# An expert layer's last weights: the same bytes from another queue, converted on chip, and a load cut in two around gathers

## The chip, the cores and the metric

One core of one Trainium2 chip. The metric is the device time of one execution in microseconds (us), the median of several executions. For one core a run is called slow when it is over 1.5% above the fastest run of the same kernel; otherwise it is fast. TensorE multiplies matrices, VectorE (DVE) and ScalarE (ACT) work on elements, GpSimd (POOL) issues most transfers here and SyncE (SP) some; PEld is TensorE's loading of weights.

## The reference

Attention first (left out here: the change does not touch it). Its 3072 rows of 512 then go through eight experts. Each computed row belongs to one expert, which is chosen by the data:

```python
xc = x[do_compute]
e_idx = np.argmax(xc @ w_gate, axis=1)
...
for e in range(E):
    mask = e_idx == e
    h = np.maximum(xc[mask] @ w1[e], 0.0)          # 512 -> 1024
    y[mask] = gate_w[mask, None] * (h @ w2[e])     # 1024 -> 512
out[do_compute] = xc + y
```

## The kernel before

A first weight `w1[e]` and a second weight `w2[e]` are 2 MiB each in fp32 in memory. TensorE wants them as fp16. The kernel before loads every one of them with a DMA issued by GpSimd that converts on the way. GpSimd also gathers the rows of an expert (indirect DMA) and scatters them back:

```python
def new_half(e, i, pool=wp, tags=("w1t", "w2t")):       # a place on chip for w1 or w2
    t = pool.tile([P, DS * F], FP16, tag=tags[i], name=tags[i])
    wts[e, i] = t.rearrange("p (s x) -> p s x", s=(DS, FS)[i])

def part(e, i, x):                                      # load a part of it, fp32 -> fp16
    nc.gpsimd.dma_start(out=wts[e, i][:, x], in_=(w1r, w2r)[i][e][:, x])
...
def in_parts(e, i, *to):                                # first half now, second half on call
    ...
def scatter(e, t):
    apart(nc.gpsimd.indirect_dma_start(out=out[:, :], ..., in_=xg[e, t], ...))
```

The work is cut into twelve units. The first eight are one tile of 128 rows of an expert among the first four. The last four are both tiles of experts 4 to 7 (counted from zero; "last expert" below is expert 7, "fourth expert" is expert 3). For each unit, `up_` multiplies by `w1` and applies the relu, and `down` multiplies by `w2`, then adds onto the gathered row with one VectorE instruction (the multiply-add, line L791):

```python
def down(n, then):
    ...
    todo = [(i, f) for i in range(len(ts)) for f in range(FS)]
    if n == len(units) - 1:                   # the last: start the second tile early
        todo = todo[:4] + todo[8:10] + todo[4:8] + todo[10:]
    for i, f in todo:
        ...
        nc.tensor.matmul(yps[i], hts[n][:, f, i * P:(i + 1) * P], wts[e, 1][:, f], ...)
    for i, t in enumerate(ts):
        nc.vector.scalar_tensor_tensor(xg[e, t], yps[i], tab[:, t, e, 1:2], xg[e, t], ...)
        waiting.append((e, t))                # to be scattered
```

The last second weights stand after unit 6, ahead of the scatters of all later units:

```python
        elif n == 2 * FB - 2:                 # after unit 6
            for x in waiting[2:]:
                scatter(*x)
            del waiting[2:]
            in_parts(7, 1)()                  # both halves of the last w2, one after the other
        elif n > 2 * FB - 2:
            scatters()
```

The softmax here doesn't subtract the row's maximum and nothing guards it: scores larger than these inputs give would overflow.

## Time and profile before

| | before |
|---|---|
| median of 3 runs | 189.2 us (188.47 to 189.75) |
| profiled run | 186.2 us, span 184.0, clock 0.978 |
| last first weights (w1t) landed, last up-projection starts: **T** | 164.97 |
| last second weights (w2t), second half in use | 171.45 = T + 6.5 |
| last matmul ends | 173.77 = T + 8.8 |
| last scatter starts | 176.04 = T + 11.1 |

A timeline line reads: start in us, length, engine, line of the kernel, operation, output and inputs, and in brackets how long the engine had been idle and what ended that. All times after "T +" are counted from the start of the last expert's up-projection, because T itself moves by several microseconds from run to run for reasons that have nothing to do with the change: three profiles of kernels that are alike up to T (before, e5 and e14 below) have 164.97, 167.16 and 169.75. One caution: the profiled run of before is a lucky one: 186.2 us, where the three others took 188.5 to 189.8. When the same file was profiled again (e5 below) its span was 187.0.

### The profile page before, as it was taken

Reading aid. Unit: us, or ns where it says so; the run is one execution under the profiler, and the core shown is the slowest. Engines: PE = TensorE matmul, PEld = TensorE weight load, DVE = VectorE, ACT = ScalarE, POOL = GpSimd, SP = SyncE. Lnnn points to the kernel's source line nnn. Section 1 sums busy time; section 2 is a strip of 40 time slices with the busy share of each in tenths; the row PEclk is TensorE's granted clock in tenths of the full one; section 3 lists DMA queues with packets and bytes.
Section 4 is the critical chain, followed back from the end, with each engine's and each line's share of the span. In section 5 each row is a group of like instructions: output and inputs, shape, how many; then the busy total and the mean of one; then the engine's idle time right before and its main releaser. Section 6 shows DMA issues by size and latency. Waiting matters only on the chain.

```text
span 184.0 us, 5757 instructions
## 1 busy us (share of the span) xinstructions
PE 160.0 (87%) x2443; PEld 113.6 (62%) x2443; DVE 105.8 (58%) x284; ACT 89.6 (49%) x138; POOL 95.2 (52%) x123
## 2 busy tenths in 40 slices
PE   5799878998978999999999999979999999999500
PEld 1464546676654887667878779657777676646100
DVE  5798938437666676687776437533565445343300
ACT  3068659896796848987448352213234332302000
POOL 7749731233761217732322891688787626507740
PEclk9999999999999999999999999999999999999965
DMA  5999999999999999999999999999999999999520
GB/s 173 169 183 164 163 192 203 200 235 138 224 208 223 237 233 211 165 220 235 252 230 240 319 253 222 203 233 253 216 244 201 202 239 251 218 251 221 182 87 2
DMA packets 53204, 38.16 MB, mean 207 GB/s; under 512 B 28448, under 2 KB 44832, under 8 KB 53168
## 3 DMA queue, kind: packets, MB, share of 16 engines
q0 software_dynamic: 49168, 30.62, 110.7%
q1 hardware_dynamic: 3728, 6.69, 10.7%
q8 instruction: 21, 0.34, 0.7%
q10 hardware_dynamic: 272, 0.39, 0.6%
q14 instruction: 15, 0.12, 0.2%
HBM read 56.66 MB, written 10.49 MB: 365 GB/s over the span
## 4 chain that ended last, share of the span: by engine, by line
PE 43%; DMA 24%; issue 11%; POOL 9%; DVE 5%; ACT 4%; POOLq 1%; DVEq 0%; ACTq 0%
DMA xg<-out_dram,idx 13%; DMA w2t<-in_moe_w_dram 8%; PE tps L307 5%; PE sps L344 4%; PE xps L468 4%; PE av L293 3%; PE sps L339 3%; PE tbp L562 3%; PE av L426 3%; DMA firstat<-in_q_dram 2%; PE sps L373 2%; POOL xg L715 2%; PE mhp L770 2%; PE av L432 2%; PE sps L404 2%
## 5 line engine op out<-in xcount | busy, mean ns | idle before, releaser
L460 POOL CAST x<-x 128x512 f16<-128x512 f32 x17 | 10.5, 619 | 38.7 <-DVE x L451 31.5
L355 ACT ACTIVATE at<-sps 128x1024 f16<-128x1024 f32 (+1 forms) x24 | 21.1, 923 | 8.7 <-PE sps L344 8.6
L788 PE MATMUL myp<-w2t,ht 128*128 128x512 f16 x96 | 23.8, 379 | 1.4 <-DMA w2t<-in_moe_w_dram 1.4
L726 POOL DMA_INDIRECT out_dram<-xg,idx x16 | 16.1, 1003 | 16.6 <-DMA out_dram<-xg,idx 4.8
L791 DVE SCALAR_TENSOR_TENSOR xg<-myp,tab,xg 128x512 f32<-128x512 f32 x16 | 12.0, 751 | 21.9 <-PE myp L788 20.2
L770 PE MATMUL mhp<-mxT,w1t 128*128 128x128 f16 (+1 forms) x320 | 22.9, 230 | 0.0
L770 PEld LDWEIGHTS <-w1t 128*128 128x128 f16 x320 | 21.0, 98 | 2.8 <-DMA w1t<-in_moe_w_dram 0.4
L776 ACT ACTIVATE ht<-mhp 128x512 f16<-128x512 f32 x16 | 9.6, 597 | 25.6 <-PE mhp L770 16.8
L720 POOL DMA_INDIRECT xg<-out_dram,idx x16 | 16.8, 1053 | 9.8 <-DVE rec L440 2.7
L788 PEld LDWEIGHTS <-ht 128*128 128x128 f16 x128 | 11.9, 98 | 12.0 <-issue 1.3
L774 DVE TENSOR_SCALAR ht<-mhp 128x512 f16<-128x512 f32 x16 | 11.0, 691 | 11.9 <-PE mhp L770 11.0
L344 PE MATMUL sps<-qT,kT 64*128 64x512 f16 (+3 forms) x96 | 14.6, 303 | 1.3 <-DVE kT L313 1.3
L394 ACT ACTIVATE ats<-sps 128x1024 f16<-128x1024 f32 (+1 forms) x16 | 12.5, 812 | 6.5 <-PE sps L385 6.5
L451 DVE TENSOR_TENSOR x<-av,rec 128x512 f32<-128x512 f32 x20 | 13.8, 692 | 1.5
L468 PE MATMUL xps<-ident,x 128*128 128x128 f16 (+1 forms) x96 | 11.3, 240 | 2.3 <-POOL x L460 1.7
L114 POOL DMA_DIRECT2D va<-in_v_dram x8 | 11.4, 1424 | 3.3 <-DMA va<-in_v_dram 2.0
L360 ACT ACTIVATE at<-sps 128x1024 f16<-128x1024 f32 (+1 forms) x12 | 10.8, 921 | 4.4 <-PE sps L344 4.3
L339 PE MATMUL sps<-tri,idl 64*128 64x128 f16 x144 | 11.5, 218 | 0.2
L293 PE MATMUL av<-esk,ident 128*128 128x512 f16 x28 | 9.4, 465 | 2.6 <-DVE ident L151 1.8
L313 DVE COPY kT<-tps 128x768 f16<-128x768 f16 x10 | 9.5, 948 | 3.6 <-PE tps L307 3.6
L313 ACT COPY qT<-tps 128x768 f16<-128x768 f16 x12 | 9.6, 797 | 3.6 <-PE tps L307 3.6
L426 PE MATMUL av<-va,at 128*128 128x65 f16 x204 | 9.9, 194 | 1.2 <-issue 1.2
(154 smaller groups left out, 343.1 us busy)
## 6 DMA issues: line engine op xcount, KB each, us to landing
out_dram<-x SPq DMA_DIRECT2D x24, 256.0 KB, 5.9
w1t<-in_moe_w_dram POOLq DMA_DIRECT2D x6, 1024.0 KB, 14.9
w2t<-in_moe_w_dram POOLq DMA_DIRECT2D x4, 1024.0 KB, 16.3
va<-in_v_dram POOLq DMA_DIRECT2D x8, 384.0 KB, 9.9
w2t<-in_moe_w_dram POOLq DMA_DIRECT2D x4, 512.0 KB, 13.4
qin<-in_moe_w_dram POOLq DMA_DIRECT2D x2, 1024.0 KB
kin<-in_moe_w_dram POOLq DMA_DIRECT2D x2, 1024.0 KB, 12.5
qin<-in_q_dram POOLq DMA_DIRECT2D x2, 768.0 KB, 9.2
```

The costliest lines, as they stand in the source:

```text
L293: nc.tensor.matmul(ps, ident, fill, start=True, stop=True)
L313: eng(t.rearrange("c (p n) -> c p n", n=NT), ps.rearrange("c n p -> c p n"))
L339: nc.tensor.matmul(ps[:, k, x:x + P], idl[rows[i], u], tri[rows[i], u], start=(u == 0), stop=False, skip_group_check=True)
L344: nc.tensor.matmul(ps[:, k, x:x + n], kT[b, pr][rows[i], j * P:(j + 1) * P], qT[b, pr][rows[i], q0:q0 + n], start=False, stop=True, skip_g ...
L355: nc.scalar.activation(both[b][:, :, o:o + w], ps[:, :, :w], ACT.Exp, scale=SCALE)
L426: nc.tensor.matmul(avo[:, 0, h // 2], at[b, h][:, x0:x0 + P], va[b % 2][:, h, j], start=False, stop=j == i, skip_group_check=True)
L451: nc.vector.tensor_tensor(x.rearrange("p c t d -> p t c d"), avo[:, :, :, :D], rec.unsqueeze(3).to_broadcast([P, 2, 4, D]), op=ALU.mult)
L468: nc.tensor.matmul(ps[:, s], x[:, s * P:(s + 1) * P], ident if x.dtype == FP16 else ident32, is_transpose=True, start=(s == 0), stop=(s == ...
L720: apart(nc.gpsimd.indirect_dma_start(out=xg[e, t], out_offset=None, in_=out[:n, :], in_offset=bass.IndirectOffsetOnAxis(ap=idx[:, t, e:e + ...
L726: apart(nc.gpsimd.indirect_dma_start(out=out[:, :], out_offset=bass.IndirectOffsetOnAxis(ap=idx[:, t, e:e + 1], axis=0), in_=xg[e, t], in_ ...
L770: nc.tensor.matmul(hp[:, u], wts[e, 0][:, s, (f0 + u) * P:(f0 + u + 1) * P], xts[n][:, s], start=(s == 0 and u == 0), stop=(s == DS - 1 an ...
L788: nc.tensor.matmul(yps[i], hts[n][:, f, i * P:(i + 1) * P], wts[e, 1][:, f], start=(f == 0), stop=(f == FS - 1))
```

## The change

The intent: take the last of the big loads off GpSimd's queue, so that SyncE's queue carries it and GpSimd is free to scatter. SyncE's load leaves the fp32 as it is, so it arrives in two pieces `w32` of 1 MiB and VectorE and ScalarE convert them in four copies of 128x1024 elements. This is **part B**. **Part A** is separate: the fourth expert's second weights are cut into two halves, and the second half is issued after two gathers instead of before them.

```diff
@@ down
-            todo = todo[:4] + todo[8:10] + todo[4:8] + todo[10:]
+            todo = todo[:4] + todo[8:12] + todo[4:8] + todo[12:]
@@ before the routing of the second tiles                      (part A)
-    for i in range(2):
-        load_half(3, i)
+    load_half(3, 0)
+    new_half(3, 1)
+    part(3, 1, slice(0, FS // 2))
@@ loop over the units
         down(n, ...)
+        if n == len(units) - 3:                                # (part B)
+            for i in range(2):
+                nc.vector.memset(w32[i][:, 0, :1], 0.0)
+                nc.sync.dma_start(out=w32[i],
+                                  in_=w2r[E - 1][:, i * FS // 2:(i + 1) * FS // 2])
         if n == len(units) - 2:
             up_(n + 1)
+            for f in range(0, FS, 2):
+                eng = nc.scalar.copy if f % 4 else nc.vector.tensor_copy
+                eng(wts[E - 1, 1][:, f:f + 2], w32[f * 2 // FS][:, f % (FS // 2):][:, :2])
         if n == 0:
             gather(0, 1)
             gather(1, 1)
+            part(3, 1, slice(FS // 2, FS))                     # (part A)
             load_half(4, 0, *qk)
@@ after unit 6
-            in_parts(7, 1)()
+            new_half(7, 1)
+            w32 = [m2.tile([P, FS // 2, DM], FP32, tag=f"w32{i}", name="w32", bufs=1)
+                   for i in range(2)]
```

## The prediction

> **What bounds the kernel now.** I read the page first (busy shares and slices), then the chain that ended last, then the timeline of the expert stage. In the page's slices TensorE and the DMA engines are both at nine tenths almost to the end, so the question is which of them sets the last microseconds:
>
> ```profile
> PE   5799878998978999999999999979999999999500
> DMA  5999999999999999999999999999999999999520
> HBM read 56.66 MB, written 10.49 MB: 365 GB/s over the span
> ```
>
> The chain that ended last, over the final 46 us, is one transfer after another and a short tail:
>
> ```profile
> 138.60 14.49 DMA xg<-out_dram,idx
> ...
> 156.30 15.11 DMA w2t<-in_moe_w_dram
> 171.41 0.04 issue
> 171.45 2.33 PE myp L788 x10
> 173.78 0.03 issue
> 173.81 0.76 DVE xg L791
> ...
> 176.04 0.98 POOL out_dram L726
> ```
>
> The reader is to see that the second half of the last expert's second weights (w2t) lands at 171.41, that ten matmuls wait for it, and that the last scatter starts 1.47 us after the final multiply-add has ended (173.81 + 0.76 = 174.57). The timeline shows the waits around this, as start, length, instruction, and in brackets the idle time before it:
>
> ```profile
> 123.69 0.63 PE L753 MATMUL mtp<-ident,xg 128*128 128x128 f32 x4 [1.34 <-DMA xg<-out_dram,idx]
> ...
> 164.97 3.39 PEld L770 LDWEIGHTS <-w1t 128*128 128x128 f16 x32 [0.42 <-DMA w1t<-in_moe_w_dram]
> ...
> 165.70 0.98 POOL L726 DMA_INDIRECT out_dram<-xg,idx  x1 [4.43 <-DMA out_dram<-xg,idx]
> ...
> 169.00 1.46 PE L788 MATMUL myp<-w2t,ht 128*128 128x512 f16 x6 [0.36 <-DMA w2t<-in_moe_w_dram]
> ...
> 171.45 2.32 PE L788 MATMUL myp<-w2t,ht 128*128 128x512 f16 x10 [1.00 <-DMA w2t<-in_moe_w_dram]
> ...
> 173.81 0.75 DVE L791 SCALAR_TENSOR_TENSOR xg<-myp,tab,xg 128x512 f32<-128x512 f32 x1 [0.54 <-PE myp L788]
> 174.75 0.98 POOL L726 DMA_INDIRECT out_dram<-xg,idx  x1 [0.31 <-DVE xg L791]
> 176.04 0.98 POOL L726 DMA_INDIRECT out_dram<-xg,idx  x1 [0.30 <-issue]
> ```
>
> Three readings. From 124 us to the end of the last up-projection TensorE hardly waits, so the 1.34 us wait at 123.69 for the gathered rows of unit (0,1) is its one sizeable gap there. GpSimd runs its last nine scatters back to back, 1.29 us apart, from 165.70 to 176.04 (8 x 1.29 = 10.3): it is itself a bound at the end. And the last expert's first weights (w1t) arrive just when TensorE wants them: issued 144.61, 20.3 us to landing in the DMA issues view, so 164.9.
>
> The DMA stream is full. After the third scatter ahead of it in the queue lands (issued 154.54, 11.8 us: 166.3), both halves of w2t land by 171.41: 2 MiB of fp32 in 5.1 us, 411 GB/s read. From the fourth expert's first weights (issued 107.09, 11.2 us, so 118.3) to w1t at 164.9 eight loads of 2 MiB are read in 46.6 us, 360 GB/s before the gathers are counted. So moving a load moves no bytes away; it changes only who goes first.
>
> A second reading of the GpSimd timeline: its DMA issues wait for the landing of the eighth DMA before them. The scatter at 153.20 follows the landing of w1t of the seventh expert (137.47 + 14.9 = 152.4), and the one at 160.24 that of the seventh's w2t (143.66 + 16.3 = 160.0).
>
> **What the Trainium skill says.** "DMA: Bandwidth & Descriptors", section "SWDGE vs HWDGE vs iDMA": a cast inside a DMA is possible only from GpSimd; hence a SyncE load must stay fp32 and be converted by an engine. The trace agrees as far as it goes: all casting loads stand on GpSimd's queue. The same page, section "Queues, rings and completion order": each DMA engine goes round its queues packet by packet, and all queues share the same 16 engines. The trace agrees: SyncE's 256 KB stores take 3.1 us to land at best and 5.9 in the median, beside GpSimd's loads. "VectorE: DVE Perf Modes", section "Mode 2x_2P": a one-source copy with both sides in SBUF gives two results a cycle even for fp32. Agreed: casting 128x512 from SBUF takes 419 ns in the median, a relu of the same shape out of PSUM 691. "ScalarE: Activation LUTs", section "What ACT_TABLE_LOAD costs": 186 ns + 0.833 ns per element, thus 1.04 us for 1024; the trace has 1.02 for 128x1024 out of PSUM and no copy out of SBUF.
>
> **The change, part by part.**
>
> (a) Fourth expert. Half of its w2t (1 MiB read, 2.5 us at 411 GB/s) moves behind two gathers. These gathers land about 2.5 us earlier than their 123.5 (116.03 + 7.5), so the 1.34 us wait goes. The half is needed only in the fourth down-projection, from 126.8; it should land near 124. The 1.3 us lead then passes on through TensorE, with the next gathers (119.81 + 9.9 = 129.7, needed by the cast at 129.86), the seventh expert's w1t (152.4, needed at 154.0) and w2t (160.0, needed at 161.4) all just soon enough. It ends at w1t of the last expert: 164.9, whatever TensorE does. **Worth at the end: nothing by itself.**
>
> (b) The GpSimd queue loses two issues at 155.5 (1.64 us) and, with them, two places in the line of eight. The scatters at 157.45, 160.24 and 165.70 can go 2 to 7 us earlier, so the back-to-back run no longer reaches the end. The last scatter then starts some 0.2 us after the last multiply-add rather than 1.47: **up to 1.2 us gained**, if TensorE's end stays at 173.78.
>
> (c) The new load starts after a VectorE memset behind the tenth unit's multiply-add (161.62 + 0.75 = 162.4; 161.1 with the lead). About 1.3 us of start-up (my choice, from a 384 KB load at the start that landed in 4.5) puts its first bytes near 162.5, while w1t still has 1.5 to 2.4 us to go. SyncE's rows are 2 KB and w1t's are 4 KB as read, so packet by packet SyncE would take about a third: w1t is stretched by half of what is left, 0.7 to 1.2 us, **to about 165.9**.
>
> (d) The conversion is added on the path. In VectorE's order the first cast stands behind the last relu, which ended at 168.68 + 0.69 = 169.4, 4.4 us after the up-projection began. A 128x1024 cast I put at 0.7 us (419 ns for 512, 555 for 768: 0.54 ns an element). So the down-projection can start 5.2 us after w1t, not at 4.0 as now: **1.2 us lost**; ScalarE's first cast, 1.05 us, runs beside it. Then 16 matmuls at 0.232 = 3.7.
>
> Sum for TensorE: 165.9 + 5.2 + 3.7 = 174.8, against 173.78. Add 0.03 + 0.76 + 0.2 for the multiply-add and the start of the scatter: **175.8 against 176.04, a gain of 0.2 us.** With w1t undelayed it is 174.8, a gain of 1.2.
>
> **Rivals.** First, the load comes late: from 162.5 there are 2 us of w1t, some seven scatters at about 0.55 us (landings 173.2, 173.9, 174.5) and 5.1 us of the load itself. If reads and writes share the DMA engines fully, the second piece lands near 173; a 1.05 us cast and six matmuls (1.4) make 175.5, and the end is 0.5 to 1 us later than before. The full DMA row speaks for it; that scatters write while loads read speaks against it. Second, SyncE gets so small a share that w1t isn't delayed while scatters are few: gain 1.2 us. Its slowed stores speak for a small share. Third, everything is hidden: TensorE's lead ends at w1t, and the tail trades GpSimd's queue for the casts: no difference. Fourth, the fp32 cast shuts GpSimd out of its port while it writes the scatters' descriptors: under 1 us, on issues that would then have slack.
>
> **Range and chances.** Of the profile's 184.0 us the arithmetic moves between -1.5 and +1.3. Its centre is -0.2; I go to -0.6, because the wait at 123.69 and GpSimd's run are plain losses now and the delay of w1t is the least certain term. On 189.2 that is 188.6 us. The three runs before span 1.3 us, so the range is 187.0 to 190.3. Two per cent is 3.8 us, more than all the waits in the last 20 us that the change touches, either way: 0.04 faster, 0.93 same, 0.03 slower.
>
> **What would show it.** (a) The wait before the transposes at 123.69 is gone, and TensorE reaches the last expert about 1.3 us sooner, to wait there for w1t. (b) The scatters after 155 start earlier and the last one follows its multiply-add within 0.3 us. (c) w1t lands between 165 and 167. (d) TensorE waits for a VectorE cast, not a DMA, before the last down-projection; the second piece lands before 172. The prediction is wrong if w1t lands at 164 or sooner (the queue really was held up elsewhere), if the second piece comes after 174, or if the lead of (a) is lost in a new wait of several microseconds.

## The result, and the profile after

The changed kernel takes 194.92 us (194.26 to 196.44, 4 runs); before takes 189.38 (the three runs above and a fourth, from the same rounds as the changed kernel). The ratio of after to before is **1.031, interval 1.024 to 1.039: slower**. Such a ratio, here and below, is the mean time of one kernel's fast runs over that of the other's of the same rounds, so not quite the ratio of the medians quoted. The profiled run has a span of 194.3 us at clock 0.972.

The page of the kernel after; these slices answer to the two shown of before. Each digit is a fortieth of the span:

```profile
PE   5899778999679998999987899996999999973500
DMA  5999999999999999999999999799999999996020
```

Before, TensorE and the DMA engines were full until the last two or three slices. Now TensorE falls to 7, 3 and 5 in slices that were 9, 9 and 5, while the DMA row is still 9 and 6: TensorE is waiting for a transfer. The 7 in the DMA row (the 26th slice, from 121 us) is new too; it is the hole made by part A, taken up below.

The chain that ended last, after, answers to the chain that ended in "15.11 DMA w2t<-in_moe_w_dram" before:

```profile
168.44 12.95 DMA w<-in_moe_w_dram
181.49 0.70 DVE w2t L881
182.24 2.38 PE myp L788 x8
184.64 0.76 DVE xg L791
```

The chain reads: the second fp32 piece ("w") came at 181.4, a copy of 0.70 us followed it, then eight matmuls, then the multiply-add. Before, the same kind of chain ended with w2t at 171.41. The timeline of the kernel after shows both sides of it:

```profile
167.59 0.07 DVE L874 MEMSET w<- 128x1 f32 x2
167.73 1.09 SPq L875 DMA_DIRECT2D w<-in_moe_w_dram  x2
...
171.28 3.67 PE L770 MATMUL mhp<-mxT,w1t 128*128 128x256 f16 x32 [1.25 <-DMA w1t<-in_moe_w_dram]
...
177.49 0.69 DVE L881 CAST w2t<-w 128x1024 f16<-128x1024 f32 x1 [1.81 <-DMA out_dram<-xg,idx]
178.24 1.89 PE L788 MATMUL myp<-w2t,ht 128*128 128x512 f16 x8 [3.29 <-issue]
...
181.49 0.69 DVE L881 CAST w2t<-w 128x1024 f16<-128x1024 f32 x1 [3.30 <-DMA w<-in_moe_w_dram]
182.24 2.37 PE L788 MATMUL myp<-w2t,ht 128*128 128x512 f16 x8 [2.11 <-DVE w2t L881]
...
184.64 0.75 DVE L791 SCALAR_TENSOR_TENSOR xg<-myp,tab,xg 128x512 f32<-128x512 f32 x1 [0.60 <-PE myp L788]
185.67 0.98 POOL L726 DMA_INDIRECT out_dram<-xg,idx  x1 [0.37 <-DVE xg L791]
```

SyncE issues the two pieces at 167.73, 3.55 us before T (171.28). The first piece is used at 177.49, the second at 181.42 (ScalarE's copy, not shown, starts there) = T + 10.1, where before had T + 6.5. TensorE stands still for 3.29 and then 2.11 us. The last scatter starts at T + 14.4; before it was T + 11.1.

T differs by 6.3 us between the two profiled runs. In the run of after, the first gathers were already issued 1.66 us later than in that of before (102.78 against 101.12), ahead of any changed instruction; that part cannot come from the change. At the next gathers, behind the first edit of part A, it is 3.36 us (119.39 against 116.03). Whether part A has a share in the rest the two profiles cannot tell; e1 below, which is part A alone, reaches T at 168.23, inside the 164.97 to 169.75 of kernels without it. The profiled run of after was the slowest of its four, and that of before the fastest of its four. So only what is counted from T is compared, and the experiments carry the rest.

### The profile page after: what moved, and what is told of

The parts are those of the page before. It is cut to its first block, busy times and chain, and to the rows that moved or that the text cites.

```text
span 194.3 us, 5767 instructions
## 1 busy us (share of the span) xinstructions
PE 161.7 (83%) x2443; PEld 113.6 (58%) x2443; DVE 107.9 (56%) x288; ACT 91.8 (47%) x140; POOL 95.0 (49%) x122
## 4 chain that ended last, share of the span: by engine, by line
PE 42%; DMA 28%; issue 9%; POOL 7%; DVE 5%; ACT 3%; POOLq 1%; SPq 0%; DVEq 0%
DMA w1t<-in_moe_w_dram 8%; DMA kin<-in_moe_w_dram 7%; DMA w<-in_moe_w_dram 7%; PE tps L307 5%; PE mhp L770 4%; PE myp L788 4%; DMA xg<-out_dram,idx 4%; PE sps L344 4%; PE av L293 3%; PE sps L339 3%; PE tbp L562 3%; PE av L426 3%; PE xps L468 2%; POOL xg L720 2%; DMA firstat<-in_q_dram 2%
## 5 line engine op out<-in xcount | busy, mean ns | idle before, releaser
L788 PE MATMUL myp<-w2t,ht 128*128 128x512 f16 x96 | 24.3, 385 | 5.5 <-issue 3.3
L355 ACT ACTIVATE at<-sps 128x1024 f16<-128x1024 f32 (+1 forms) x24 | 21.1, 922 | 9.2 <-PE sps L344 9.2
L788 PEld LDWEIGHTS <-ht 128*128 128x128 f16 x128 | 11.9, 99 | 16.3 <-issue 6.4
L791 DVE SCALAR_TENSOR_TENSOR xg<-myp,tab,xg 128x512 f32<-128x512 f32 x16 | 12.0, 751 | 14.3 <-PE myp L788 11.9
L756 ACT COPY mxT<-mtp 128x512 f16<-128x512 f16 x11 | 6.2, 587 | 11.4 <-PE mtp L753 9.9
```

Of the source, the lines that this page charges most:

```text
L355: nc.scalar.activation(both[b][:, :, o:o + w], ps[:, :, :w], ACT.Exp, scale=SCALE)
```

## The experiments

Fourteen kernels ran, all with correct results, in four calls (e1 to e4, e5 to e8, e9 to e12, e13 and e14), each on another chip, so that a time is compared only with the runs of before in its own call. "One look" means a single run, whose state is unknown. The theory after reading the two traces: **the load stands in the wrong place**. Behind the tenth unit's multiply-add it starts only some 3 us before T, and it shares the DMA engines with the last first weights and then with the scatters. The rivals: the hole in the DMA row made by part A; the fp32 form and the four copies; TensorE's clock, which falls when it waits; and plain luck of the profiled runs.

| run | what | median us (before in its call) | ratio, interval |
|---|---|---|---|
| e1_a_only | part A alone | 190.57 (190.5) | 1.002 [0.998, 1.006] |
| e2_b_only | part B alone | 195.06 (190.5) | 1.024 [1.019, 1.029] |
| e3_a_split | part A's halves, not moved | 190.26 (190.5) | 1.001 [0.997, 1.006] |
| e4_a_fed | part A, hole filled | 190.42 (190.5) | 1.002 [0.997, 1.006] |
| e5_before_again | before, profiled again | 189.16 (190.41) | one look |
| e6_b_hold | B, scatters meant to be held | 194.75 (190.41) | one look |
| e7_b_mid | B, load one unit sooner | 195.67 (190.41) | 1.026 [1.019, 1.033] |
| e8_late_pool | before's load at B's place | 194.4 (190.41) | 1.012 [1.001, 1.023] |
| e9_b_hold2 | B, scatters really held | 197.91 (188.57) | one look |
| e10_b_fill | B, TensorE kept busy | 193.36 (188.57) | 1.033 [1.027, 1.038] |
| e11_first | before, load ahead of three scatters | 189.78 (188.57) | 1.011 [1.006, 1.015] |
| e12_first_whole | the same, in one piece | 191.07 (188.57) | 1.015 [1.008, 1.023] |
| e13_gp_fp32 | B, but GpSimd's queue and before's place | 190.49 (190.6) | 1.001 [0.997, 1.005] |
| e14_order | before, only the matmul order | 190.91 (190.6) | 1.006 [1.002, 1.011] |

In the call of e10 to e12 two lucky runs of before (185.77 and 185.82), and in that of e13 and e14 one (186.95), leave only 9 of 18 and 11 of 35 of its runs fast, because a run counts as fast only near the fastest. The ratios there lie 0.1 to 0.7 per cent above those of the medians, which are 1.025, 1.006, 1.013, 0.999 and 1.002.

### Part A alone (e1, e3, e4)

```diff
e1, against before
-    for i in range(2):
-        load_half(3, i)
+    load_half(3, 0)
+    new_half(3, 1)
+    part(3, 1, slice(0, FS // 2))
...
             gather(1, 1)
+            part(3, 1, slice(FS // 2, FS))
e3, against e1: that second part() stands right behind the first instead
e4, against e1: half of the next expert's first weights is loaded in its place
```

> The kernel before with only the fourth expert's second weights in halves around the two gathers. Theory 'dry queue': in the changed kernel's trace the DMA engines' share falls to 0.55, 0.23, 0.55 and 0.88 between 121 and 125 us, where the kernel before holds 1.1 to 1.3, because half as many bytes stand in GpSimd's queue while the routing is computed; the stage is bound by its DMA, so about 2.5 us should be lost to the end: ratio 1.010 to 1.016, and the same hole in the DMA share. Rival 'it is all the last load': part (a) is free or gains up to 1.3 us, ratio 0.993 to 1.003, and the changed kernel's loss lies in part (b). Rival 'the profile caught a slow start': no hole in this trace.

> The kernel before with the fourth expert's second weights in two halves, both still ahead of the routing: one DMA more on GpSimd's queue, no bytes moved. Theory 'dry queue': no hole in the DMA share, ratio 0.997 to 1.004. Rival 'one more DMA in the line of eight delays the issues after it': the loss of e1_a_only is here as well, 1.01.

> As e1_a_only, but half of the fifth expert's first weights (1 MiB read) is issued ahead of the routing in place of the half that moved away, and its other half behind the gathers: as many bytes in the queue as before, and the split still around the gathers. Theory 'dry queue': the hole is filled and the loss of e1_a_only goes, ratio 0.996 to 1.005. Rival 'the gathers or the later half come too late in this order': the loss stays at about 1.01.

The hole is there in e1: the DMA share falls to 0.51 in the window from 120 to 122 us. It costs nothing that the times show, 1.002, against an expected 1.010 to 1.016. e3 and e4 agree with it to a tenth of a per cent. The dry-queue theory fell. The last up-projection then starts at 168.23 with the usual T + 6.4 for the second half: what part A does in the middle is absorbed on the way, as the prediction had said for another reason.

### Part B alone (e2)

```diff
e2, against after: part A undone
-    load_half(3, 0)
-    new_half(3, 1)
-    part(3, 1, slice(0, FS // 2))
+    for i in range(2):
+        load_half(3, i)
...
-            part(3, 1, slice(FS // 2, FS))
```

> The changed kernel with the fourth expert's weights as before: only the SyncE fp32 load, the casts and the order of the last matmuls. Theory: the load is issued only behind the tenth unit's multiply-add and takes 13 us to land; against the kernel before, whose second half lands 6.5 us after the last first weights, it lands 10 us after them; less what GpSimd's queue gives back, 3 to 3.5 us are lost: ratio 1.015 to 1.020. If both theories hold, the two ratios minus one add up to the changed kernel's 3.1 per cent. Rival 'it is all part (a)': 0.995 to 1.004.

Measured 1.024: part B carries the loss, a little more of it than I expected. A and B together make 1.026; the interval of the change's 1.031 (1.024 to 1.039) holds this. The timeline of e2:

```profile
163.99 1.09 SPq L874 DMA_DIRECT2D w<-in_moe_w_dram  x2
...
167.13 3.67 PE L770 MATMUL mhp<-mxT,w1t 128*128 128x256 f16 x32 [0.23 <-DMA w1t<-in_moe_w_dram]
...
174.58 2.86 PE L788 MATMUL myp<-w2t,ht 128*128 128x512 f16 x8 [3.78 <-DVE w2t L880]
177.58 1.04 ACT L880 CAST w2t<-w 128x1024 f16<-128x1024 f32 x1 [2.75 <-DMA w<-in_moe_w_dram]
...
178.39 3.57 PE L788 MATMUL myp<-w2t,ht 128*128 128x512 f16 x8 [0.95 <-DVE w2t L880]
```

The same picture as after: issued 3.1 us before T, second piece in use at T + 10.5. T itself, 167.13, is not later than in before's second profile (167.16). Since T moves from run to run, the time from the issue of the last first weights to T says more: 20.7 to 21.6 us in the five kernels with SyncE's load in part B's place (after, e2, e6, e9, e10), mean 21.1, and 19.5 to 21.7 in eight that load through GpSimd alone (before, e1, e3, e4, e5, e8, e13, e14), mean 20.7. If SyncE's load delayed them, it was by some 0.4 us, less than the spread. The last matmuls take 3.57 us for eight instead of 1.89: half clock, see e10.

The packets of the load, counted from the trace's DMA records ("SyncE" is the load, "GpSimd" are packets of 1 KB and more of the other queue):

```
             first    half     90%     last     took
after        169.01  174.06  177.30  180.85   11.8 us
e2_b_only    165.29  170.30  173.54  177.21   11.9 us
e9_b_hold2   164.23  168.72  171.09  173.52    9.3 us

after, packets per us     169  170  171  172  173  174  175  176  177  178  179  180
  SyncE, 2 KB each         11   73  128  145  160  173  131   79   56   34   28    6
  GpSimd                   74   53   32   21   19   12   21   17   16   27   12   10
```

Two things stand out. SyncE's queue is not shut out by the other: from 172 to 176 it moves 6 to 14 packets for one of GpSimd's. (By bytes it is half of that: from 171 on GpSimd's packets are the scatters' and have 4 KB. Only 22 packets of the first weights came after the load's first packet.) But the last tenth of the load, some 100 packets, takes 3.6 us, nearly a third of the whole. In that tail the DMA engines have room: their mean share is 0.95 in the microsecond from 175, then 0.63, 0.51, 0.48, 0.30 and 0.14. So the late packets do not wait for a full stream; it looks as if a few engines had more left than the others, which these records do not show.

### Before, profiled again (e5)

No edit: the file of before.

> The kernel before, unchanged, for a second profile of it: the first one was of a run of 186.2 us, below each of its other runs (188.5 to 192.8). Theory 'the first profile was a lucky run': the span is 186.5 to 189, and the last multiply-add waits some 2 us past its last matmul, as it does in the three profiles of e1, e3 and e4 and not in the first of before. Rival: it shows the tail of the first profile again, 0.5 us of wait.

```profile
167.16 3.67 PE L770 MATMUL mhp<-mxT,w1t 128*128 128x256 f16 x32 [1.11 <-DMA w1t<-in_moe_w_dram]
...
173.51 2.32 PE L788 MATMUL myp<-w2t,ht 128*128 128x512 f16 x10 [0.99 <-issue]
...
177.98 0.75 DVE L791 SCALAR_TENSOR_TENSOR xg<-myp,tab,xg 128x512 f32<-128x512 f32 x1 [2.66 <-remote]
```

The second half again comes 6.4 us after T, but T is 2.2 us later than in the first profile of before: that one was lucky. A surprise stands in the third line. The last matmul ended at 175.83, yet the last multiply-add starts 2.15 us later, and the profile names only "remote". The same wait, 1.85 to 2.8 us, is in e1, e3, e4, e13 and e14; it is not in before's first profile, nor in e8, e11 and e12, which also load through GpSimd, nor in any kernel that loads through SyncE. What it waits for stays open.

### Holding the scatters (e6, e9)

```diff
e6, against e2: the scatters of the last units come after the last unit
-        elif n > 2 * FB - 2:
+        elif n == len(units) - 1:
             scatters()
e9, against e6: and GpSimd must first read converted weights
+            held = m1.tile([P, DM], FP16, tag="held", name="held", bufs=1)
+            nc.gpsimd.tensor_copy(held, wts[E - 1, 1][:, FS - 2])
             scatters()
```

> As e2_b_only, but all scatters from the eighth unit on are held until the last unit is done, so that no scatter runs beside the SyncE load (the time itself must get longer: eleven scatters, 1.29 us apart, at the end). Theory 'the scatters hold back some of the DMA engines': in e2 nine tenths of the load's packets are through 8 us after its first and the last tenth takes 4 us more; here the last piece should land 7 to 8.5 us after the first packet instead of 12, and within 7.5 us of the last first weights instead of 10.5. Rival 'the SyncE load is slow by itself': 11 us or more again.

> A second try at e6, where the scatters weren't held, because GpSimd is free and does not wait for the place in the program. Here GpSimd copies one row of the converted weights first, and so waits for the last cast; eleven scatters come after it, and the time gets longer by some 12 us. Theory 'the scatters hold back some of the DMA engines': the fp32 load's last packet comes 7 to 9 us after its first instead of 12 to 12.6 (e2, e6), and within 7.5 us of the last first weights. Rival 'the SyncE load is slow by itself, or its engines are uneven from the start': 11 us or more.

e6 failed as an experiment: GpSimd has nothing else to do and ran the scatters beside the load just as before, so moving them in the program held nothing. Its load took 12.6 us. In e9 they are held for certain. The timeline of e9:

```profile
163.08 1.09 SPq L874 DMA_DIRECT2D w<-in_moe_w_dram  x2
...
167.31 3.67 PE L770 MATMUL mhp<-mxT,w1t 128*128 128x256 f16 x32 [1.44 <-DMA w1t<-in_moe_w_dram]
...
174.00 1.05 ACT L880 CAST w2t<-w 128x1024 f16<-128x1024 f32 x1 [1.56 <-DMA w<-in_moe_w_dram]
```

From first to last packet the load takes 9.3 us instead of 11.9, near the 7 to 9 us that the theory of shared engines expected, and the second piece is in use at T + 6.7, within its 7.5. With scatters beside it the load took 11.8 to 13.3 us in four profiles (after, e2, e6, e10). So **the scatters of the other queue cost this load some 2.6 us**, half of it in the last tenth (2.4 us instead of 3.7), by one profile with them held. Of the 3.8 us between T + 6.7 and e2's T + 10.5 the other 1.2 us is that here the first packet came 3.1 us before T and in e2 1.8. The kernel as a whole is slower, 197.91, because eleven scatters now follow the end: it shows a cause and is no remedy.

### The load sooner (e7)

```diff
e7, against e2
-        if n == len(units) - 3:
+        if n == len(units) - 4:
             for i in range(2):
                 nc.vector.memset(w32[i][:, 0, :1], 0.0)
```

> As e2_b_only, but the SyncE load is issued one unit sooner (some 7 us). Theory 'the bytes are conserved': the fp32 load then takes its bandwidth from the last first weights, which land 3 to 5 us later in relation to the stage; the casts are done before they are needed, no wait for the load is left, and the loss of e2 shrinks but does not go: ratio 1.008 to 1.018. Rival 'the load only came late': the loss goes, 0.995 to 1.004.

The expectation missed in size: 1.026, no better than e2. The load now runs from 161.89 to 176.05 and is in time, but (this profile is of a slow run):

```profile
158.34 1.09 SPq L874 DMA_DIRECT2D w<-in_moe_w_dram  x2
...
167.97 3.61 PE L788 MATMUL myp<-w2t,ht 128*128 128x512 f16 x16 [2.69 <-DMA w2t<-in_moe_w_dram]
...
175.76 5.33 PE L770 MATMUL mhp<-mxT,w1t 128*128 128x256 f16 x32 [4.18 <-DMA w1t<-in_moe_w_dram]
```

The waits have moved to the weights of GpSimd's queue: 2.69 us for the seventh expert's second weights and 4.18 us for the last first weights. In a full DMA stream bytes that go first make others go later, as the prediction says of moves; here the sooner start on the second queue only moved the wait to other weights. From 162 to 166 us, while both queues carry weights and no scatter, the trace has 281 packets of each: one for one, SyncE's of 2 KB, GpSimd's of 2 KB (206) or 1 KB (75) as written, and twice that as read.

### The late place with the old load (e8)

```diff
e8, against before
+        if n == len(units) - 3:
+            in_parts(7, 1)()
...
-            in_parts(7, 1)()      # after unit 6
```

> The kernel before, with its casting load of the last second weights by GpSimd moved to the place where the changed kernel issues SyncE's load, behind the tenth unit; no fp32, no cast on an engine. Theory 'issued late, and so behind the scatters and the last first weights': it waits in GpSimd's queue and for its place in the line of eight, lands 8 to 9 us after the last first weights, ratio 1.008 to 1.018: half or more of e2's loss without a fp32 load. Rival 'the loss is SyncE's, from fp32 and the casts': 0.997 to 1.005.

Here nothing is fp32 on chip and no copies are added; only the place is late. 1.012 with only two fast runs of six, and a median 2% above before's. In the profile (a slow run):

```profile
169.23 1.62 POOL L125 DMA_DIRECT2D w2t<-in_moe_w_dram  x2
...
178.60 4.21 PE L788 MATMUL myp<-w2t,ht 128*128 128x512 f16 x10 [1.65 <-DMA w2t<-in_moe_w_dram]
```

The halves are issued 1.6 us after T (167.59), where SyncE's load stood 3.1 to 3.6 us ahead of it, and the second is in use at T + 11.0. So a late load costs time without fp32 and copies too: by the estimate half of part B's loss, but the interval reaches from nearly none of it to all.

### Does the falling clock matter? (e10)

```diff
e10, against e2, last down-projection: matmuls nobody reads keep TensorE busy
+            busy = mhp.tile([P, 512], FP32, tag="mh", name="mhp")
+            fills(13, busy)
+        for k, (i, f) in enumerate(todo):
+            if n == len(units) - 1 and k == 8:
+                fills(8, busy)
```

> As e2_b_only, with 13 dummy matmuls ahead of the last down-projection and 8 in its middle, in the time in which TensorE waits for the load and the casts. Theory 'the idle TensorE loses its clock': in the profiles of e2 and e6 the granted clock fell to 0.5 some 4 us into that wait and the last 16 matmuls took 0.4 us instead of 0.22; here it stays at 1.0 to the last matmul, and 1 to 2.5 us come back: ratio 1.008 to 1.020 against the kernel before, and below e2's 1.024. Rival 'the clock is a matter of the profiled runs only': 1.022 to 1.027.

"TensorE: Matmul & The Clock Gate", section "HAM oscillation", warns of TensorE gaps beyond some 3.4 us, after which the clock halves. The runs agree in part: e2 waits 3.78 us and its clock is 0.5 from 175.3 on; the profiled run of after waits 3.29 us and keeps full clock. But it then waits only 2.11 us, up to 182.24, and its clock is 0.5 from 183.5 on: here a shorter gap was enough. In e10 the clock stays at 1.0 and the eight last matmuls take 1.89 us, not 3.57. Yet the expectation missed: the ratio is 1.033, by the medians 1.025, and not below e2's 1.024. So no part of the loss is shown to come from the clock. Why the gain in the profile is not in the times stays open; one difference is that e10's load took 13.3 us where e2's took 11.9.

### Earlier on GpSimd's queue (e11, e12)

```diff
e11, against before
+            in_parts(7, 1)()
             for x in waiting[2:]:
                 scatter(*x)
             del waiting[2:]
-            in_parts(7, 1)()
e12: the same with load_half(7, 1), one DMA, in place of in_parts(7, 1)()
```

> The kernel before with its two loads of the last second weights issued ahead of the three scatters of the seventh unit instead of behind them. Theory 'the end is bound by the order of the DMA queue': both halves land 1.4 us sooner after the last first weights, the matmuls' waits of 0.4 and 1.0 us go, and up to 1.2 us are gained where GpSimd's run of scatters allows: ratio 0.993 to 1.000. Rival 'GpSimd's run of scatters is the bound': 0.999 to 1.003.

> As e11_first, but the two halves as one load: one place less in GpSimd's line of eight, so the run of scatters that follows the last first weights is one shorter (1.29 us). Theory 'GpSimd's run of scatters is the bound, and the queue's order comes second': ratio 0.991 to 0.998, below e11. Rival 'the matmuls that wait for the whole load lose as much': 0.999 to 1.005.

If the place in the queue matters, a better place than before's might win. It does not, and both expectations of a gain missed (1.011 and 1.015). The timeline of e11 after T = 166.99:

```profile
170.25 0.98 POOL L726 DMA_INDIRECT out_dram<-xg,idx  x1 [1.56 <-DVE ht L774]
170.49 3.91 PE L788 MATMUL myp<-w2t,ht 128*128 128x512 f16 x16
...
174.44 0.75 DVE L791 SCALAR_TENSOR_TENSOR xg<-myp,tab,xg 128x512 f32<-128x512 f32 x1 [0.55 <-PE myp L788]
...
180.55 0.98 POOL L726 DMA_INDIRECT out_dram<-xg,idx  x1 [0.30 <-issue]
```

TensorE no longer waits and is done at T + 7.4, better than before's T + 8.8. But the scatters now stand behind the load, GpSimd stalls twice by 1.56 us among them (the second stall, at 172.81, is not shown) and its last scatter starts 6.1 us after the last multiply-add does. In e12 the stall is one of 4.08 us. GpSimd's run of scatters, which the prediction named as a bound of its own, sets the end here.

### Queue or copies? (e13), and the order of the matmuls (e14)

```diff
e13, against e2: GpSimd loads the fp32 pieces where before issues its load
-        if n == len(units) - 3:
-            for i in range(2):
-                nc.vector.memset(w32[i][:, 0, :1], 0.0)
-                nc.sync.dma_start(out=w32[i], in_=...)
...
             w32 = [...]               # after unit 6
+            for i in range(2):
+                nc.gpsimd.dma_start(out=w32[i], in_=...)
e14, against before
-            todo = todo[:4] + todo[8:10] + todo[4:8] + todo[10:]
+            todo = todo[:4] + todo[8:12] + todo[4:8] + todo[12:]
```

> Part B with one thing taken back: the two fp32 pieces of the last second weights are loaded by GpSimd's queue, at the place in the program where the kernel before issues its casting load, and are then converted by the same four copies. Queue-and-place theory (the loss comes from the load standing on SyncE's queue behind the tenth unit, not from fp32 or the copies): the second piece lands 6 to 7 us after the last first weights, the last scatter starts about 12.5 us after them, and the time is 1.000 to 1.007 of before, against 1.024 for part B. Rival (fp32 on chip and the copies carry a good part of the loss): 1.012 or more, with TensorE waiting over 1.5 us for the copies after the pieces have landed.

> The kernel before with only the order of the last sixteen matmuls changed as in the change (four of the second tile ahead instead of two). Expected 0.997 to 1.003 of before: the ten matmuls that wait for the second half become eight, 0.5 us less at TensorE, but the last scatters are held by GpSimd's line and not by TensorE. If the last matmuls set the end, 0.997 or a little less.

e13 is the decisive one. It keeps the fp32 pieces, the four copies and the new matmul order, and gives back only the queue and the place:

```profile
159.69 1.62 POOL L913 DMA_DIRECT2D w<-in_moe_w_dram  x2
...
168.84 3.67 PE L770 MATMUL mhp<-mxT,w1t 128*128 128x256 f16 x32 [1.18 <-DMA w1t<-in_moe_w_dram]
...
174.50 3.82 PE L788 MATMUL myp<-w2t,ht 128*128 128x512 f16 x16 [1.99 <-ACT w2t L875]
175.47 1.05 ACT L875 CAST w2t<-w 128x1024 f16<-128x1024 f32 x1 [1.61 <-DMA w<-in_moe_w_dram]
```

The loss is gone: 1.001 [0.997, 1.005] against 1.024. (Set against all 11 fast runs of before in the call, and not only those of the same rounds, it is 1.007.) The second piece is in use at T + 6.6, as in before, although the same scatters go out; most of them now stand behind it in the one queue. The rival's sign did show: TensorE waits 1.99 us, and the first copies end that wait. But the copies cost little of it in the end: the last matmul ends at T + 9.5 instead of T + 8.7 (e5), some 0.8 us later, and in the median nothing of it is seen.

Is it the queue or the place that e13 gives back? e7 helps: its SyncE load was issued at 158.34, about when e13's GpSimd issued the same pieces (159.69), and e7 still lost 2.6 per cent. So at neither of the two places that were tried was SyncE's queue free of the loss; for GpSimd's queue e8 shows that a late place costs too.

e14: 1.006 [1.002, 1.011] by the ratio, above the expected band, and 1.002 by the medians, inside it; its profile is of a slow run. The order of the last matmuls is no gain; if it has a part in the loss, it is a small one.

No version beat both kernels.

## Why the prediction was wrong

I predicted 188.6 us and 93% for no difference beyond 2%; the change costs 3.1%.

**The step that failed is the sum for TensorE, 165.9 + 5.2 + 3.7: it has no term for waiting for the load.** In step (d) the down-projection waits for a copy behind the last relu and then runs through; the load was to be there "before 172", that is T + 6.1 with the predicted T of 165.9. The runs show a load that sets the end: the second piece is in use at T + 10.1 (after) and T + 10.5 (e2), TensorE stands still twice before it is through (3.29 and 2.11 us in after), and it ends at T + 13.3 instead of T + 8.9.

The mechanism had been named, as the first rival, "the load comes late", and was set aside because scatters write while loads read. Its size was too small as well: it put the second piece "near 173", T + 7, and the end "0.5 to 1 us later". Its sum from the first bytes to the last was 2 + 3.9 + 5.1 = 11 us, and the load took 11.8 (after) and 11.9 us (e2). So its length was nearly right, and the missing 3 us lie in these places (in after):

- *The start.* The rival counts from 162.5, 3.4 us before the predicted T. The first packet came 2.3 us before T (in e2 1.8): 1.1 us.
- *The length*, 0.9 us. The parts of its sum were off both ways: with the scatters held, what is left (the load and the last first weights) takes 9.3 us (e9) and not 7.1, and the scatters add some 2.6 us and not 3.9. "5.1 us of the load itself" was read off GpSimd's stream with all DMA engines at work; in the tail of this load they are not, and its last tenth takes 2.4 us even with the scatters held.
- *From the last packet to the copy*, 0.6 us (180.85 to 181.42), and 0.5 us by which the sum was rounded down to "near 173".

Step (c) missed as well, without harm: the first weights were to be stretched by 0.7 to 1.2 us, and some 0.4 us is the most that the profiles show. The share that it gave to SyncE, "about a third", is not what was wrong: where the two queues did carry weights side by side (e7) the packets went one for one, so SyncE had 37% of the bytes read. But in after only 22 packets of the first weights were left when the load began.

By its other steps:

- **(a)** Right in worth, "nothing by itself" (e1: 1.002), and wrong in the picture: it did not see that the queue would run dry around 121 us. The expected mark came: the wait before the transposes of unit (0,1), 1.34 us in before and 0.62 in e5, is gone in e1 (at 123.90) and in after (at 125.73). But the lead did not reach the last expert as forecast; other waits follow, of 0.66 us in e1 (at 133.13) and 1.62 us in after (at 135.86, where VectorE had waited 2.81 us for gathered rows).
- **(b)** Right in the trace and without worth. In after the last scatter follows its multiply-add by 0.28 us (185.67 against 184.64 + 0.75), where 0.3 had been the mark. The three scatters that were to go 2 to 7 us earlier go 1.3, 2.8 and 7.0 us earlier, counted from T. But GpSimd's freedom gains nothing when TensorE is over 4 us late.
- **(d)** Right for the copies and for what stands ahead of them, and wrong where it says that nothing else is waited for: VectorE's copy was put at 0.7 and took 0.69 us, ScalarE's at 1.05 and took 1.04, and the last relu ended at T + 4.4 in after, as forecast. But the first copies began only at T + 6.2, with the first piece. In e13, where the load is in time, the down-projection starts at T + 5.7 against the T + 5.2 put down. The fourth rival, that VectorE's copy hinders GpSimd's scatters, is small: scatters beside such a copy took 0.99 us in e2, 1.15 in after and 1.25 in e10, and 0.98 otherwise.
- The prediction's own sign of failure, "if the second piece comes after 174", is what came about (181.4, and 177.6 in e2). The range was too tight because it took the last 20 us' waits of *before* as the measure of what could be lost; a new wait is not bounded by old ones.

What stays open: which DMA engines hold the late packets of the load (the records used do not tell), and so why its tail is long; the wait of about 2 us ahead of the last multiply-add in six profiles of GpSimd-loading kernels (it hides part of part B's lateness: TensorE ends 6.2 us later in e2 than in e5, counted from T, but the last scatter starts only some 4 us later); and how the loss divides between the queue and the late start.

## What to carry to other kernels

In this full DMA stream the one queue was also an order of service: with the load ahead of most scatters in it the second piece was in use at T + 6.6 (e13), and from a second queue at T + 10.5 (e2), though the load was neither larger nor starved. So before moving the last transfer that something waits for, look at what stands behind it in its old queue, date its start on the new queue from the instruction that releases it, and time it by the share it will have, not by the rate of the old stream.

## What the Trainium skill lacked or had wrong

- "DMA: Bandwidth & Descriptors", section "Queues, rings and completion order": it gives the round of the queues by packets of 9 to 17 descriptors, but not what share a converting GpSimd load and a SyncE load then get of each other. In e7, from 162 to 166 us, the trace has 281 packets of each, SyncE's of 2 KB and most of GpSimd's of 4 KB as read.
- "TensorE: Matmul & The Clock Gate", section "HAM oscillation": it warns of gaps beyond some 3.4 us. In after the clock was 0.5 from 183.5 on, behind a gap of 2.11 us.
- No page that I read says that scatters of another queue stretch a large load's end. Here they add some 2.6 us to a load of 2 MiB (11.9 us in e2 against 9.3 in e9), and the last tenth of its packets takes 3.7 us against 2.4 with the scatters held.
